# Two transposes of an adaLN, attention and gated-FFN kernel, moved from matrix products to DMA transposes

## The chip, the cores and the metric

The kernel runs on one core of one Trainium2 chip. The metric is device microseconds (us) of one execution; three runs of the kernel before are shown. One more execution was taken by the hardware profiler, and every row below is from it.

## The reference

One transformer block over 2048 rows of 512 numbers: attention of 32 heads that share one key and one value head of 16 numbers, then a bilinear gated unit of width 1792, each behind a layer norm whose scale and shift come from a conditioning vector `c`.

```python
mod = (_silu(c) @ w_mod).reshape(c.shape[0], 6, 1, -1)
sa, ca, ga, sb, cb, gb = (mod[:, 0], mod[:, 1], mod[:, 2], mod[:, 3], mod[:, 4], mod[:, 5])
h = _layernorm(x, axis=-1) * (1 + ca) + sa
x = x + ga * _A_ref(h, A_wq, A_wk, A_wv, A_wo)
h = _layernorm(x, axis=-1) * (1 + cb) + sb
x = x + gb * _B_ref(h, B_w_gate, B_w_up, B_w_down)
...
scores = jnp.einsum("bhqd,bkd->bhqk", q, k) * (Dh ** -0.5)
p = _softmax(scores, axis=-1)
...
g = jnp.einsum("bsd,df->bsf", x, w_gate)
u = jnp.einsum("bsd,df->bsf", x, w_up)
h = g * u
return jnp.einsum("bsf,fd->bsd", h, w_down)
```

## The kernel before

Attention is cut into 32 units: 8 blocks of 256 rows (called sb) by 4 groups of 8 heads. A unit has 16 turns, one for each 128 keys. In a turn TensorE makes four score products (`sc`, lines 657 and 659), ScalarE takes four exponentials of 128x512 (line 661), and TensorE then multiplies them with the values in eight products (`pv`, line 670; these eight open a row of the timeline, so the distance between two such rows is the length of a turn). Every product that keeps numbers exact enough is split into fp16 halves, high and low.

A softmax needs each row's maximum before its exponentials. So the scores are made twice: first as `mx` products (line 601), four in a turn, each reduced by VectorE to a maximum (line 605, `mpart`). These run ahead: 30 steps of maxima are taken before the first exponential (`LEAD`), two more steps go with every turn, and unit u needs its first 24 + 32u. So the last maximum of a unit is taken six steps, three turns, ahead of that unit's first score. In between lies a chain, here called the chain of the maxima: `max_fin` reduces to `mm` (128x16, line 622); `max_rows` turns `mm` by a product with the identity (line 629), splits it in fp16 halves on ScalarE and VectorE (lines 634, 635) and sends it by two small DMAs into rows 48 and 49 of each half of the unit's stationary tile `sst` (line 639).

The linear layers are worked off beside attention, as side groups (line 511): q projections, then for each block of rows the output projection `wo_work`, the gate and up products of `ffn_work` (14 groups with one output tile each) and the down products. A turn takes 4 or 8 half-height side products (the orders `FEW` and `MANY`) or none (`NO_SIDE`, where no group may start). What is not done when attention ends is done behind it, at full height.

`wo_work` ends each 128-row tile by adding x, and by the second norm: statistics on VectorE, the inverse deviation on GpSimd, and `nrm`, which writes the normalised rows `n2` (by GpSimd for blocks 2 to 5, line 769; by ScalarE else, line 771). `ln2_work` then turns `n2` by eight 128x128 products with the identity, four to a turn (line 805), lets ScalarE apply scale and shift, which now are per partition (`hf`, line 813), and lets GpSimd split in halves into `h2T` (lines 818, 819; VectorE for the last block). Only then is block sb put into `h2done`, and only then may its ffn groups start.

Order: each engine runs its instructions in program order, and the program is written in ticks, two to a turn; `after(n, f)` writes f's instructions n ticks later. SyncE (SP) issues all DMAs in one such order; an issue that waits for its data holds up those behind it.

Of the kernel before, what the change touches and what calls it, by code (L numbers as in the profile page):

```python
# [16 lines left out]
OP = mybir.AluOpType  # L17
# [14 lines left out]
SQ_GAP = 2.6  # L32
LAG = 2
ROW_LAG = 4
SLOTS = (0, 1, 2, 3, 6, 7)
SUM_GAP = 4.0
SUM_LAG = 3
SPLIT_GAP = 2.5
# [3 lines left out]
NBANK = 8  # L42
QPRE = 24
Q_LAG = 8
TR_WAIT = 11
NHF = 12
M_STEP = 23
PAIRED = 14
# [15 lines left out]
def adaln_mqa_glu_kernel(ctx: ExitStack, tc: tile.TileContext, x_in, wq_in, wk_in, wv_in, wo_in,  # L64
# [159 lines left out]
    kwb = big.tile([128, 2 * FT * D], F16, name="kwb", tag="wd")  # L224
    hfs = kwb[:, 0:2 * NHF * BT].bitcast(F32).rearrange("p (n t) -> p n t", n=NHF)
    ssqs = [kwb[:, 2 * n * BT:2 * n * BT + 2 * F].bitcast(F32) for n in (KC, 2 * KC)]
    kng = kwb[:, 2 * NHF * BT:2 * NHF * BT + BT]

    def hf(b, k):
# [390 lines left out]
    def max_fin(u):  # L620
        mms[u] = work.tile([128, 2, 8], F32, name="mm")
        nc.vector.tensor_reduce(mms[u], mparts[u], axis=AX.X, op=OP.max)

    def max_rows(u):
        def f():
            mms[u, "b"] = ps_hold("mxt")
            p = mms[u, "b"][0:16, 0:128]
            mms[u, "p"] = p
            nc.tensor.transpose(p, mms[u].rearrange("p a c -> p (a c)"), ident)  # L629

        def g():
            p = mms[u, "p"]
            mt = [work.tile([16, 128], F16, name=f"mt{hl}") for hl in range(2)]
            nc.scalar.activation(mt[0], p, AF.Copy, scale=1.0 / 32.0)
            nc.vector.scalar_tensor_tensor(mt[1], p, 1.0 / 32.0, mt[0], op0=OP.mult, op1=OP.subtract)
            ps_give(mms[u, "b"])
# [85 lines left out]
            timers.setdefault(tick[0] + delay, []).append(f)  # L722

    x1s = {}
    n2s = {}
    n2f = {}

    def load_x(t):
# [6 lines left out]
    def wo_work(sb):  # L735
        on_pool = 2 <= sb < NS - 2

        def op(t):
            def f(i):
                ch, term = divmod(i, 3)  # L740
                ol, wl = TERMS[term]
                return [(och[sb, ch][:, ol, t * 128:(t + 1) * 128], wo[:, wl, ch, :])]
            return f

        def fin(t):
            row = 2 * sb + t

            def f(p):
                x1 = x1s[row]
                nc.vector.scalar_tensor_tensor(x1, p, sca[:, 7:8], x1, op0=OP.mult, op1=OP.add)  # L750
                s2 = work.tile([128, 1, 2], F32, name="st2", bufs=5)
                bs = work.tile([128, 6], F32, name="bs", bufs=4)
                nb = work.tile([128, 2], F32, name="nb", bufs=4)
                yt = {}

                def spread():
                    nc.vector.bn_stats(bs, x1)

                def aggr():
                    nc.vector.bn_aggr(s2[:, 0, :], bs)  # L760
                    yt["y"] = rstd_of(s2, 1)
                    if not on_pool:
                        nc.gpsimd.tensor_tensor(nb[:, 0:1], s2[:, 0, 0:1], yt["y"], op=OP.mult)
                        nc.gpsimd.tensor_scalar(nb[:, 1:2], nb[:, 0:1], -1.0, 0.0, op0=OP.mult, op1=OP.add)

                def nrm():
                    n2 = work.tile([128, D], F32, name="n2", tag="n2", bufs=2)
                    if on_pool:
                        nc.gpsimd.tensor_scalar(n2, x1, s2[:, 0, 0:1], yt["y"], op0=OP.subtract, op1=OP.mult)
                    else:  # L770
                        nc.scalar.activation(n2, x1, AF.Identity, bias=nb[:, 1:2], scale=yt["y"])
                    n2s[row] = n2

                after(3, spread)
                after(4, aggr)
                n2f[row] = nrm
                if t == 1:
                    late = 3 if sb < 2 else 0
                    for j in range(2):
                        after((4, 9)[j] + late, n2f[2 * sb + j])  # L780
                    if sb < NS - 1:
                        after(TR_WAIT + late, lambda: turns.extend(ln2_work(sb)))
# [6 lines left out]
    turns = deque()  # L789
    glus = []  # L790

    def ln2_work(sb):
        st = {}

        def tr(i):
            def f():
                if not h2s:
                    h2T = big.tile([128, 2, 2, KC, ST], F16, name="h2T", tag="wq")
                    glus.append(big.tile([128, 2, 2, FT, ST], F16, name="glu", tag="big"))
                    h2s.update({s: h2T[:, s % 2] for s in range(NS)})  # L800
                st["p"] = ps_hold("mx")
                for k in range(2):
                    for t in range(2):
                        c = k * ST + t * 128
                        nc.tensor.transpose(st["p"][:, c:c + 128],  # L805
                                            n2s[2 * sb + t][:, (2 * i + k) * 128:(2 * i + k + 1) * 128], ident)
            return f

        def ev(i):
            def f():  # L810
                hf = work.tile([128, 2, ST], F32, name="hf", tag="g", bufs=2)
                for k in range(2):
                    nc.scalar.activation(hf[:, k, :], st["p"][:, k * ST:(k + 1) * ST], AF.Identity,  # L813
                                         bias=hsc[:, 2 * i + k, 0:1], scale=hsc[:, 2 * i + k, 1:2])
                ps_give(st["p"])
                eng = nc.vector if sb == NS - 1 else nc.gpsimd
                h = h2s[sb][:, :, 2 * i:2 * i + 2, :]
                eng.tensor_scalar(h[:, 0], hf, 1.0, 0.0, op0=OP.mult, op1=OP.add)
                eng.tensor_tensor(h[:, 1], hf, h[:, 0], op=OP.subtract)
                if i == 1:  # L820
                    (after if sb == 0 else lambda d, f: f())(3, lambda: h2done.add(sb))
            return f

        return [(900, tr(i), ev(i)) for i in range(2)]

    W = {}
    hsc = consts.tile([128, KC, 2], F32, name="hsc")
# [65 lines left out]
    def late_weights():  # L893
# [16 lines left out]
        def m2():  # L910
            st["p"] = ps_mx()
            mod_cols(st["row"][0:64, :], modT[1], st["p"])
            md = dram.tile([2, D], F32, name="md")
            nc.sync.dma_start(md, st["row"][64:128:32, :])
            st["md"] = md

        gab = work.tile([128, D], F32, name="gab", tag="x1", bufs=6)
        gbb = consts.tile([128, D], F32, name="gbb")

        def m3():  # L920
            nc.sync.dma_start(gab, st["md"][0:1, :].to_broadcast([128, D]))
            nc.sync.dma_start(gbb, st["md"][1:2, :].to_broadcast([128, D]))

        items = []
        sl = list(wslices())
# [5 lines left out]
        def stage(n):  # L931
            if "d" in W:
                t = work.tile([128, D], F32, name="wsl", tag="xl", bufs=3)
            else:
                t = hfs[:, SLOTS[taken[0] % len(SLOTS)], :]
                taken[0] += 1
            nc.sync.dma_start(t[:, :sl[n][3]], sl[n][2])
            st[n] = t
# [94 lines left out]

        def inverse():
            nc.vector.reciprocal(sca[:, 0:5], st["t"][:, 0:5])
            nc.vector.tensor_scalar(hsc, modT[1][:, :, 0:64:32], sca[:, 4:5], None, op0=OP.mult)
            nc.gpsimd.tensor_scalar(gab, gab, sca[:, 3:4], 0.0, op0=OP.mult, op1=OP.add)

        def last_column():
# [73 lines left out]

    wlist, dlist, mod_rows = late_weights()
    NSTEP = 32
    later = {}
    mstep = [0, 0]

    def drain_posts():
# [8 lines left out]
    def max_half(a):  # L1128
# [14 lines left out]
            max_parts(u + 1)  # L1143
        if last:
            max_fin(u)
            (_, f, g), = max_rows(u)
            later[min(mstep) + 1] = (f, g)

    def late_max():
        for at in [m for m in later if m <= min(mstep)]:  # L1150
            f, g = later.pop(at)
            f()
            posts.append(g)
            return True
        return False

# [27 lines left out]
    qs = deque(q_proj(b, ch) for b in range(NB) for ch in ((2, 3, 0, 1) if b == 0 else range(KC)))  # L1184
    for n in range(LEAD):
        drain_posts()
        late_max()
# [30 lines left out]
    def attend(u, kt):  # L1218
# [10 lines left out]
        def end_turn(kt):  # L1229
# [7 lines left out]
            if v >= 0:  # L1237
                pv(*divmod(v, KT))
                if v % KT == KT - 1:
                    ends.append(lambda: pv_out(u - 1))  # L1240
            if not late_max() and turns and all(q.ended() for q in qs):
                _, f, post = turns.popleft()
                f()
                posts.append(post)
            hooks(u, 2 * kt + 1)

        for turn in range(2):
# [4 lines left out]
            for j, (what, a) in enumerate(order):  # L1252
                if j == len(order) // 2:
                    drain_posts()
                    if style is not NO_SIDE:
                        late_max()
# [103 lines left out]


# [15 lines left out]
```

## Time and profile before

| what | value |
|---|---|
| median of 3 runs | 1665.59 us (1664.72 to 1666.26) |
| span of the profiled execution | 1663.8 us |
| what lies around the span, against the median | 1.8 us |
| TensorE matmul busy | 1643.3 us, 99% |
| VectorE busy | 1402.3 us, 84% |
| ScalarE busy | 1234.8 us, 74% |
| GpSimd busy | 523.5 us, 31% |
| share of the chain that ended last | PE 93%, ACT 2%, DVE 2%, DMA 1% |

The page gives the span of the profiled execution, from its first to its last instruction; its time as the runs are timed is not shown, and is put here at the span and the 1.8 us. Engines: PE is TensorE, DVE VectorE, ACT ScalarE, POOL GpSimd, SPq the DMA issues of SyncE. Busy time of PE counts overlapping products once.

### The profile page before, as it was taken

How to read it: one execution, taken by the hardware profiler on the slowest of the kernel's cores; microseconds unless marked ns; L12 is line 12 of the kernel's file. 1: busy time of each engine (PE TensorE's matmuls, PEld its weight loads, DVE VectorE, ACT ScalarE, POOL GpSimd, SP SyncE). 2: the span in 40 equal slices, each digit the busy share in tenths (PEclk: the TensorE clock that was granted, in tenths of full speed). 3: DMA queues.
4: the chain of work that ended last, by engine and by line, in shares of the span. 5: the costliest groups of instructions: out<-in, count | busy, mean ns of one | idle time of the engine just before them, and what ended most of it. 6: DMA issues, size and time to landing. Idle time of an engine off the chain costs nothing.

```text
span 1663.8 us, 39821 instructions
## 1 busy us (share of the span) xinstructions
PE 1643.3 (99%) x15677; PEld 747.1 (45%) x15677; DVE 1402.3 (84%) x2434; ACT 1234.8 (74%) x2389; POOL 523.5 (31%) x833
## 2 busy tenths in 40 slices
PE   8899999999999999999999999999999999999999
PEld 4333333355533554335543355434545345454776
DVE  7999999998998999899998999999998999980211
ACT  5688888888777877777877787777878777877300
POOL 4857537864841111301112011300113001210322
PEclk9999999999999999999999999999999999999999
DMA  6313313342210001000000000000000000000100
GB/s 237 108 59 100 95 43 120 96 129 80 77 51 24 18 12 32 19 32 20 20 26 23 25 13 24 26 25 26 20 29 15 26 22 20 26 14 21 33 13 14
DMA packets 66024, 75.39 MB, mean 45 GB/s; under 512 B 17702, under 2 KB 46634, under 8 KB 65836
## 3 DMA queue, kind: packets, MB, share of 16 engines
q1 hardware_dynamic: 63724, 72.26, 13.7%
q8 instruction: 123, 2.02, 0.5%
q10 hardware_dynamic: 2112, 0.59, 0.1%
q14 instruction: 65, 0.53, 0.1%
HBM read 55.51 MB, written 17.04 MB: 44 GB/s over the span
## 4 chain that ended last, share of the span: by engine, by line
PE 93%; ACT 2%; DVE 2%; DMA 1%; issue 1%; POOL 0%; SPq 0%; ACTq 0%; DVEq 0%
PE side L511 41%; PE pv L670 30%; PE mx L601 8%; PE sc L659 8%; PE sc L657 3%; ACT P L661 2%; DVE mpart L605 1%; DMA xbig<-in_A_x_dram 1%; PE mx L805 1%; PE mxt L629 0%; ACT hf L813 0%; PE sc L601 0%; DVE bs L248 0%; DMA kwb<-in_B_w_down_dram 0%; DMA wkv<-in_A_wv_dram 0%
## 5 line engine op out<-in xcount | busy, mean ns | idle before, releaser
L605 DVE TENSOR_REDUCE mpart<-mx 128x1 f32<-128x512 f32 x2016 | 1274.1, 684 | 104.0 <-PE mx L601 95.7
L661 ACT ACTIVATE P<-sc 128x512 f32<-128x512 f32 x2048 | 1094.8, 598 | 274.2 <-PE sc L659 226.9
L601 PE MATMUL mx<-kst,sst 48*128 48x512 f16 x2032 | 631.5, 377 | 3.8 <-ACT P L661 1.7
L659 PE MATMUL sc<-sst,kst 50*128 50x512 f16 x1792 | 597.5, 379 | 0.6 <-ACT P L661 0.3
L670 PE MATMUL pv<-P,vst 128*32 128x512 f32 x4096 | 545.3, 605 | 0.7
L511 PE MATMUL side<-h2T,wg 64*128 64x256 f16 (+1 forms) x2396 | 540.8, 271 | 0.1
L511 PE MATMUL side<-h2T,wu 64*128 64x256 f16 (+1 forms) x2396 | 538.7, 270 | 0.0
L511 PEld LDWEIGHTS <-wg 64*128 64x128 f16 (+1 forms) x2396 | 226.0, 94 | 230.5 <-ACT P L661 194.0
L511 PE MATMUL side<-wd,glu 64*128 64x512 f16 (+1 forms) x1172 | 272.8, 378 | 0.2 <-ACT P L661 0.2
L850 POOL TENSOR_SCALAR glu<-gf 128x256 f16<-128x256 f32 x112 | 45.8, 409 | 671.3 <-DVE gf L849 583.9
L511 PEld LDWEIGHTS <-wu 64*128 64x128 f16 (+1 forms) x2396 | 226.4, 94 | 43.0 <-issue 7.8
L601 PEld LDWEIGHTS <-sst 48*128 48x128 f16 x2064 | 189.9, 94 | 34.2 <-issue 17.4
L659 PEld LDWEIGHTS <-kst 50*128 50x128 f16 x1792 | 162.9, 94 | 63.0 <-issue 50.3
L511 PEld LDWEIGHTS <-glu 64*128 64x128 f16 (+1 forms) x1172 | 98.5, 94 | 192.4 <-ACT P L661 85.9
L670 PEld LDWEIGHTS pv<-P,vst 128*32 128x32 f32 x4096 | 80.7, 108 | 160.9 <-issue 150.1
L849 DVE TENSOR_TENSOR gf<-side,g 128x256 f32<-128x256 f32 x112 | 46.7, 418 | 79.8 <-ACT g L847 77.7
L657 PE MATMUL sc<-sst,kst 50*128 50x256 f16 x512 | 96.9, 268 | 0.1
L511 PE MATMUL side<-h,wq 64*128 64x512 f16 (+1 forms) x372 | 95.0, 376 | 0.4 <-ACT P L661 0.4
L847 ACT ACTIVATE g<-side 128x256 f32<-128x256 f32 x112 | 42.3, 379 | 65.6 <-PE side L511 65.3
L511 PE MATMUL side<-wo,och 64*128 64x512 f16 (+1 forms) x360 | 86.3, 377 | 0.0
L851 POOL TENSOR_TENSOR glu<-gf,glu 128x256 f16<-128x256 f32 x112 | 75.3, 673 | 9.3
L706 POOL TENSOR_TENSOR oc<-oc,rr 128x256 f32<-128x256 f32 x31 | 22.7, 731 | 146.6 <-DMA rr<-ri 100.4
(233 smaller groups left out, 865.4 us busy)
## 6 DMA issues: line engine op xcount, KB each, us to landing
pd<-ev SPq DMA_DIRECT2D x32, 256.0 KB
kwb<-in_B_w_gate_dram SPq DMA_DIRECT2D x32, 224.0 KB
kwb<-in_B_w_up_dram SPq DMA_DIRECT2D x32, 224.0 KB
sst<-qd SPq DMA_DIRECT2D x180, 32.0 KB
qd<-q SPq DMA_DIRECT2D x16, 256.0 KB
oc<-pd SPq DMA_DIRECT2D x64, 64.0 KB
rr<-ri SPq DMA_DIRECT2D x64, 64.0 KB
x<-in_A_x_dram SPq DMA_DIRECT2D x14, 256.0 KB
```

The costliest lines, as they stand in the source:

```text
L511: return nc.tensor.matmul(self.p[:, c * w:(c + 1) * w], left[rows], right[rows], start=start and c == 0, stop=stop and c == len(terms) - 1)
L601: nc.tensor.matmul(m, s[64 * a:64 * a + 48, t // 2, p, t % 2 * 128:(t % 2 + 1) * 128], w[64 * a:64 * a + 48, :], start=(i == 0), stop=(i = ...
L605: nc.vector.tensor_reduce(part, m, axis=AX.X, op=OP.max)
L657: nc.tensor.matmul(t[:, c * ST:(c + 1) * ST], keys, s[64 * a:64 * a + 50, c, p, :], start=True, stop=True)
L659: nc.tensor.matmul(t.rearrange("k (c n) -> k c n", c=2), keys, s[64 * a:64 * a + 50, :, p, :], start=True, stop=True)
L661: ex = nc.scalar.activation(ptl[u, kt, p, a], t, AF.Exp)
L670: nc.tensor.matmul(pvb[u][32 * j:32 * j + 32, :], vst[:, kt, :], ptl[u, kt, p, a], start=(kt == 0), stop=(kt == KT - 1))
L706: eng.tensor_tensor(o, o, st["r"], op=OP.mult)
L847: nc.scalar.activation(g, p[:, 0:ST], AF.Copy, scale=2.0 ** -45)
L849: nc.vector.tensor_tensor(gf, p[:, ST:2 * ST], g, op=OP.mult)
L850: nc.gpsimd.tensor_scalar(glu()[:, 0, f, :], gf, 1.0, 0.0, op0=OP.mult, op1=OP.add)
L851: nc.gpsimd.tensor_tensor(glu()[:, 1, f, :], gf, glu()[:, 0, f, :], op=OP.subtract)
```

## The change

The rows of the second norm are scaled and shifted as they lie, with the scale and shift spread over all partitions (`cbb`, `sbb`, two more broadcast loads), and split in halves, by GpSimd (VectorE for the last block); the halves of 128 rows (128x1024, fp16) are then turned by one DMA transpose straight into `h2T`. `mm` is split in halves by VectorE and turned by one DMA transpose of 128x128 (32 columns used), from where the two small DMAs go on. No product, no ScalarE instruction and no PSUM bank is left in either. Two of six staging slots for weights move, and the scratch for software DMAs shrinks.

```diff
-SLOTS = (0, 1, 2, 3, 6, 7)
+ROWS_LAG = 2
+SLOTS = (0, 1, 2, 3, 12, 13)
...
-TR_WAIT = 11
+TR_LAG = 4
+H2_LAG = 3
...
     def max_rows(u):
-        def f():
-            mms[u, "b"] = ps_hold("mxt")
-            p = mms[u, "b"][0:16, 0:128]
-            mms[u, "p"] = p
-            nc.tensor.transpose(p, mms[u].rearrange("p a c -> p (a c)"), ident)
-
-        def g():
-            p = mms[u, "p"]
-            mt = [work.tile([16, 128], F16, name=f"mt{hl}") for hl in range(2)]
-            nc.scalar.activation(mt[0], p, AF.Copy, scale=1.0 / 32.0)
-            nc.vector.scalar_tensor_tensor(mt[1], p, 1.0 / 32.0, mt[0], op0=OP.mult, op1=OP.subtract)
-            ps_give(mms[u, "b"])
+        m, c = mms[u].rearrange("p a c -> p (a c)"), mtc[:, u % 2, :]
+        nc.vector.tensor_scalar(c[:, 0:16], m, 1.0 / 32.0, None, op0=OP.mult)
+        nc.vector.scalar_tensor_tensor(c[:, 16:32], m, 1.0 / 32.0, c[:, 0:16], op0=OP.mult, op1=OP.subtract)
+        t = mtT[:, u % 2, :]
+
+        def rows():
             s = sst[u % 3]
             for hl in range(2):
-                nc.sync.dma_start(s[48 + hl:113 + hl:64].rearrange("p c q n -> p (c q n)"), mt[hl])
-        return [(100, f, g)]
+                nc.sync.dma_start(s[48 + hl:113 + hl:64].rearrange("p c q n -> p (c q n)"), t[16 * hl:16 * hl + 16, :])
+
+        after(1, lambda: nc.sync.dma_start(t, c, transpose=True))
+        after(1 + ROWS_LAG, rows)
...
+                    eng = nc.vector if sb == NS - 1 else nc.gpsimd
                     if on_pool:
-                        nc.gpsimd.tensor_scalar(n2, x1, s2[:, 0, 0:1], yt["y"], op0=OP.subtract, op1=OP.mult)
+                        eng.tensor_scalar(n2, x1, s2[:, 0, 0:1], yt["y"], op0=OP.subtract, op1=OP.mult)
                     else:
                         nc.scalar.activation(n2, x1, AF.Identity, bias=nb[:, 1:2], scale=yt["y"])
-                    n2s[row] = n2
+                    eng.tensor_tensor(n2, n2, cbb, op=OP.mult)
+                    eng.tensor_tensor(n2, n2, sbb, op=OP.add)
+                    n16 = work.tile([128, 2, D], F16, name="n16", tag="gf", bufs=4)
+                    eng.tensor_scalar(n16[:, 0, :], n2, 1.0, 0.0, op0=OP.mult, op1=OP.add)
+                    eng.tensor_tensor(n16[:, 1, :], n2, n16[:, 0, :], op=OP.subtract)
+                    after(TR_LAG + (3 if sb < 2 else 0), lambda: ln2_turn(sb, t, n16))
...
-    def ln2_work(sb):
...
+    def ln2_turn(sb, t, n16):
...
+        to = h2s[sb].rearrange("p l k n -> p (l k) n")[:, :, t * 128:(t + 1) * 128]
+        nc.sync.dma_start(to, n16.rearrange("p l d -> p (l d)"), transpose=True)
+        if t == 1:
+            after(H2_LAG + (3 if sb < 2 else 0), lambda: h2done.add(sb))
...
-            if not late_max() and turns and all(q.ended() for q in qs):
-                _, f, post = turns.popleft()
-                f()
-                posts.append(post)
...
     run(wo_work(NS - 1))
-    cover(6000)
-    run_items(ln2_work(NS - 1))
     cover(1e9)
```

ScalarE's order in unit 17 (the turn of block 3 falls into it), before: the exponentials `P` of line 661 with what stands between them, up to the unit's evacuation `ev`.

```order
L661 ACTIVATE P<-sc 128x512 x28
L847 ACTIVATE g<-side 128x256
L661 ACTIVATE P<-sc 128x512 x12
L813 ACTIVATE hf<-mx,hsc 128x256 x2
L661 ACTIVATE P<-sc 128x512 x4
L813 ACTIVATE hf<-mx,hsc 128x256 x2
L661 ACTIVATE P<-sc 128x512 x4
L634 ACTIVATE mt_15014<-mxt 16x128
L661 ACTIVATE P<-sc 128x512 x16
L676 ACTIVATE ev<-pv,evs 128x512
```

The same unit of the change, whose line 664 is the exponentials and line 829 `g`:

```order
L664 ACTIVATE P<-sc 128x512 x24
L829 ACTIVATE g<-side 128x256
L664 ACTIVATE P<-sc 128x512 x12
L829 ACTIVATE g<-side 128x256
L664 ACTIVATE P<-sc 128x512 x12
L829 ACTIVATE g<-side 128x256
L664 ACTIVATE P<-sc 128x512 x16
L679 ACTIVATE ev<-pv,evs 128x512
```

The five instructions between exponentials that served the two transposes are gone; the `g` of the side groups have moved by a few turns.

SP's order of DMA issues at the same place, before: the loads of the quotients (`oc`, `ri`, `rr`), of the q rows for a later unit (`sst<-qd`) and of the maxima of unit 18 (`sst<-mt`).

```order
L690 DMA oc<-pd_14409 64x1x256 x2
L695 DMA ri_14634<-rc 128x16
L700 DMA rr<-ri_14634 64x1x256 x2
L566 DMA sst_129<-qd_3_3796 16x4x256 x6
L639 DMA sst_128<-mt_15014 2x8x128
L639 DMA sst_128<-mt_15015 2x8x128
L679 DMA pd_15178<-ev 128x512
```

And of the change:

```order
L693 DMA oc<-pd_14237 64x1x256 x2
L698 DMA ri_14482<-rc 128x16
L703 DMA rr<-ri_14482 64x1x256 x2
L803 DMA_TRANSPOSE h2T<-n_14478 128x8x128
L569 DMA sst_129<-qd_3_3787 16x4x256 x6
L803 DMA_TRANSPOSE h2T<-n_14623 128x8x128
L642 DMA_TRANSPOSE mtT<-mtc 128x128
L640 DMA sst_128<-mtT 2x8x128 x2
L682 DMA pd_15056<-ev 128x512
```

Two transposes of `h2T`, which wait for GpSimd, now stand ahead of the q rows and of the maxima, and the maxima's two DMAs stand behind a transpose of their own.

Where block 0's ffn groups may start (`h2done`), the change writes it five ticks later: eight turns of order `NO_SIDE` instead of four stand there, and with four fewer `MANY` turns 32 half-height side products go behind attention.

## Rows read from the trace of the kernel before

**Rows 1.** The page, part 1: busy us, share of span, instructions.

```profile
PE 1643.3 (99%) x15677; PEld 747.1 (45%) x15677; DVE 1402.3 (84%) x2434; ACT 1234.8 (74%) x2389; POOL 523.5 (31%) x833
```

**Rows 2.** Window, one block: length, PE, PEld, DVE, ACT, POOL busy, PEclk, DMA share, GB/s.

```profile
617.86:805.03 187.17, 187.01 (x1868) 82.85 (x1865) 171.37 (x288) 146.35 (x280) 30.80 (x54) 1.00 0.08 23
```

**Rows 3.** Timeline of PE around block 2's turn: start us, duration us, engine, line.

```profile
685.97 1.07 PE L670 MATMUL pv<-P,vst 128*32 128x512 f32 x8
688.81 1.06 PE L670 MATMUL pv<-P,vst 128*32 128x512 f32 x8
689.80 0.65 PE L805 MATMUL mx<-ident,n 128*128 128x128 f32 x4
692.58 1.06 PE L670 MATMUL pv<-P,vst 128*32 128x512 f32 x8
```

**Rows 4.** Groups by line: busy us, mean ns of one | idle before, releaser.

```profile
L813 ACT ACTIVATE hf<-mx,hsc 128x256 f32<-128x256 f32 x32 | 16.2, 561 | 9.9 <-PE mx L805 9.7
L635 DVE SCALAR_TENSOR_TENSOR mt<-mxt,mt 16x128 f16<-16x128 f32 x32 | 8.8, 276 | 2.8 <-ACT mt L634 2.6
```

**Rows 5.** Timeline of PE in the last turns before unit 29.

```profile
1403.76 1.07 PE L670 MATMUL pv<-P,vst 128*32 128x512 f32 x8
1404.76 0.28 PE L629 MATMUL mxt<-ident,mm 128*16 128x128 f32 x1
1406.81 1.06 PE L670 MATMUL pv<-P,vst 128*32 128x512 f32 x8
1409.72 1.07 PE L670 MATMUL pv<-P,vst 128*32 128x512 f32 x8
```

**Rows 6.** Timeline of PE in the last turns before unit 3, beside q projections.

```profile
194.43 1.06 PE L670 MATMUL pv<-P,vst 128*32 128x512 f32 x8
197.27 1.07 PE L670 MATMUL pv<-P,vst 128*32 128x512 f32 x8
199.77 1.06 PE L670 MATMUL pv<-P,vst 128*32 128x512 f32 x8
```

**Rows 7.** Timeline of PE in the four turns without side work.

```profile
310.02 1.06 PE L670 MATMUL pv<-P,vst 128*32 128x512 f32 x8
312.49 1.06 PE L670 MATMUL pv<-P,vst 128*32 128x512 f32 x8
...
321.47 1.07 PE L670 MATMUL pv<-P,vst 128*32 128x512 f32 x8
```

**Rows 8.** Timeline of PE behind attention.

```profile
1578.44 1.04 PE L805 MATMUL mx<-ident,n 128*128 128x128 f32 x8
...
1579.31 0.27 PE L511 MATMUL side<-h2T,wg 128*128 128x256 f16 x1
...
1579.42 0.27 PE L511 MATMUL side<-h2T,wu 128*128 128x256 f16 x1
```

**Rows 9.** Timelines of DVE and SP: the chain of the maxima of unit 29.

```profile
1403.93 0.22 DVE L622 TENSOR_REDUCE mm<-mpart 128x16 f32<-128x64 f32 x1
...
1405.36 1.19 SPq L639 DMA_DIRECT2D sst<-mt  x2
```

**Rows 10.** Timeline of SP: a store of 256 KB and the load that waits for it.

```profile
1137.41 0.34 SPq L679 DMA_DIRECT2D pd<-ev  x1
1139.42 0.57 SPq L686 DMA_DIRECT2D rc<-pd  x1
```

**Rows 11.** The chain that ended last: its longest DMA inside attention (start, length).

```profile
393.53 4.23 DMA kwb<-in_B_w_down_dram
```

**Rows 12.** Groups by line, GpSimd.

```profile
L769 POOL TENSOR_SCALAR n<-x,st,ry 128x512 f32<-128x512 f32 x8 | 16.7, 2084 | 0.0
L819 POOL TENSOR_TENSOR h2T<-hf,h2T 128x512 f16<-128x512 f32 x14 | 16.3, 1163 | 1.2
```

**Rows 13.** Timelines of POOL and DVE in block 3: norm, and unit 18's `mm`.

```profile
874.85 2.09 POOL L769 TENSOR_SCALAR n<-x,st,ry 128x512 f32<-128x512 f32 x1
...
891.92 0.22 DVE L622 TENSOR_REDUCE mm<-mpart 128x16 f32<-128x64 f32 x1
```

More of the change, by code (lines that the diff above doesn't have):

```diff
@@ L226, in adaln_mqa_glu_kernel @@
     ssqs = [kwb[:, 2 * n * BT:2 * n * BT + 2 * F].bitcast(F32) for n in (KC, 2 * KC)]
+    stg = kwb.bitcast(F32).rearrange("p (n t) -> p n t", t=BT)
     kng = kwb[:, 2 * NHF * BT:2 * NHF * BT + BT]
@@ L780, in f @@
                         after((4, 9)[j] + late, n2f[2 * sb + j])
-                    if sb < NS - 1:
-                        after(TR_WAIT + late, lambda: turns.extend(ln2_work(sb)))
             return f
@@ L788, in adaln_mqa_glu_kernel @@
     h2done = set()
-    turns = deque()
     glus = []
-    def ln2_work(sb):
[L793 to L824, printed above, removed]
+    def ln2_turn(sb, t, n16):
+        if not h2s:
+            h2T = big.tile([128, 2, 2, KC, ST], F16, name="h2T", tag="wq")
+            glus.append(big.tile([128, 2, 2, FT, ST], F16, name="glu", tag="big"))
+            h2s.update({s: h2T[:, s % 2] for s in range(NS)})
+        to = h2s[sb].rearrange("p l k n -> p (l k) n")[:, :, t * 128:(t + 1) * 128]
+        nc.sync.dma_start(to, n16.rearrange("p l d -> p (l d)"), transpose=True)
+        if t == 1:
+            after(H2_LAG + (3 if sb < 2 else 0), lambda: h2done.add(sb))
     W = {}
-    hsc = consts.tile([128, KC, 2], F32, name="hsc")
+    cbb = consts.tile([128, D], F32, name="cbb")
+    sbb = consts.tile([128, D], F32, name="sbb")
     cmx = consts.tile([128, 6], F32, name="cmx")
@@ L912, in m2 @@
             mod_cols(st["row"][0:64, :], modT[1], st["p"])
-            md = dram.tile([2, D], F32, name="md")
-            nc.sync.dma_start(md, st["row"][64:128:32, :])
+            md = dram.tile([4, D], F32, name="md")
+            nc.sync.dma_start(md, st["row"][0:128:32, :])
             st["md"] = md
@@ L920, in m3 @@
         def m3():
-            nc.sync.dma_start(gab, st["md"][0:1, :].to_broadcast([128, D]))
-            nc.sync.dma_start(gbb, st["md"][1:2, :].to_broadcast([128, D]))
+            for j, t in enumerate((sbb, cbb, gab, gbb)):
+                nc.sync.dma_start(t, st["md"][j:j + 1, :].to_broadcast([128, D]))
         items = []
@@ L934, in stage @@
             else:
-                t = hfs[:, SLOTS[taken[0] % len(SLOTS)], :]
+                t = stg[:, SLOTS[taken[0] % len(SLOTS)], :]
                 taken[0] += 1
@@ L1035, in inverse @@
             nc.vector.reciprocal(sca[:, 0:5], st["t"][:, 0:5])
-            nc.vector.tensor_scalar(hsc, modT[1][:, :, 0:64:32], sca[:, 4:5], None, op0=OP.mult)
+            nc.gpsimd.tensor_scalar(cbb, cbb, sca[:, 4:5], sca[:, 4:5], op0=OP.mult, op1=OP.add)
+            nc.gpsimd.tensor_scalar(sbb, sbb, sca[:, 4:5], 0.0, op0=OP.mult, op1=OP.add)
             nc.gpsimd.tensor_scalar(gab, gab, sca[:, 3:4], 0.0, op0=OP.mult, op1=OP.add)
@@ L1115, in adaln_mqa_glu_kernel @@
     NSTEP = 32
-    later = {}
     mstep = [0, 0]
@@ L1145, in max_half @@
             max_fin(u)
[L1146 to L1151, printed above, removed]
-            f()
-            posts.append(g)
-            return True
-        return False
+            max_rows(u)
     fill = deque()
@@ L1254, in attend @@
                     drain_posts()
-                    if style is not NO_SIDE:
-                        late_max()
                     hooks(u, 2 * (kt + turn))
```

8 lines of the change are left out of this document (4 added, 4 removed).

## The prediction

> **What bounds the kernel now.** The page first: TensorE is busy 1643 us of 1664 [rows 1], so whatever leaves its path without putting a wait there comes off the time. Busy time of pipelined products is no proof, so I cut the span into blocks. Over one block of four units TensorE is busy 187.0 of 187.2 us and VectorE 171.4 [rows 2]: VectorE has 8% of room, ScalarE 22%, GpSimd 84%. The timeline then shows the unit of account, the turn: from one `pv` row to the next 2.84 us [rows 3]. A turn that holds four products of the second norm's turn is 3.77 us long (688.81 to 692.58), and one with the maxima's product is 3.05 us (1403.76 to 1406.81) [rows 3, 5]. Where few or no side products stand, a turn is 2.47 to 2.50 us [rows 6, 7]. The sum below is of such differences.
>
> The profiled span is 1663.8 us; the median of the runs is 1665.6. I make the sum against the span and add the 1.8 us that lie between.
>
> **The second norm's turn.** Blocks 1 to 6 have two such turns each, 12 in all. Four products alone are not 0.93 us: they begin at 689.80 and are modelled for 0.65 us [rows 3]. The rest is ScalarE: two `hf` evacuations of 561 ns [rows 4] stand in its order between the exponentials, so the next values products wait for their exponentials. Both leave with the change, and the turn should fall to 2.84: 12 x 0.93 = 11.2 us. Nothing comes back on TensorE or ScalarE.
>
> Behind attention the last block's eight products open a gap of 0.87 us between side products (1578.44 to 1579.31) [rows 8]. Side products of block 6 stand behind it in plenty: eight gate and up groups of 24 products and two down groups, and the former alone, at 0.11 us a product [rows 8], are 21 us of cover for VectorE's eight instructions (each 1.2 us at most by GpSimd's row, under 10 us [rows 12]) and a transpose. So 0.9 us, with nothing given back.
>
> Block 0 differs. Its two turns fall among four turns without side work, which take 11.45 us together (310.02 to 321.47); one without products takes 2.47 [rows 7]. The change writes eight such turns, and four full ones (2.91 us at most as read in [rows 5], 1406.81 to 1409.72) fewer. Before: 11.45 + 4 x 2.91 = 23.1 us. After: 8 x 2.47 = 19.8 us, and 32 half-height side products later on, which behind attention are 16 full-height pairs, 16 x 0.22 = 3.5 us: 23.3 us. A loss of 0.2 us.
>
> **The maxima's turn.** Of 32 units, 27 have it in a turn of full length: 3.05 - 2.84 = 0.21 us each, 5.7 us. Four early ones, beside q projections, cost 0.34 us (2.84 against 2.50) [rows 6]. There VectorE sets the turn, and the change leaves it two small instructions where it had one (276 ns [rows 4]); the gain there is between nothing and 1.4 us, I take 0.7. Unit 0's lies ahead of attention, and I give it nothing.
>
> **What is added.** VectorE: per unit one more instruction of 16 columns, 0.28 us by the row of its like [rows 4], 9 us over the kernel, in turns where it waits for TensorE anyhow; less 171.4 + 1.1 of 184.5 us a block. GpSimd: per 128 rows three more 512-column instructions, less its share of the old split. By [rows 12] a tile takes 2.08 us and four times 1.16 us, 6.7 us, two tiles 13.4 us in a block of 187 us; nothing waits for it early, since from block 1 on the order has the former block's groups between: 43 ticks or more, some 60 us at half a turn each, from the last tile of `wo_work` to the block's first ffn group. Two more broadcast loads, the two small GpSimd instructions and the moved staging slots lie ahead of attention or in GpSimd's idle time: nothing.
>
> **The one cost that the trace does not show** is the DMA transpose, call it L from issue to landing. It decides through the chain of the maxima. For unit 29: `mm` starts at 1403.93 [rows 9]; with its 0.22 us and two small instructions at 0.28, the halves are ready at 1404.7. Then L, then the two small DMAs, whose issues take 1.19 us together (the second starts 0.6 after the first) [rows 9], and landing, 2.0 us by the row of a store and its dependent load [rows 10]. So the rows stand at 1407.3 + L. The unit's first score comes behind the `pv` of 1409.72, 1.0 us after its start as the product of 1404.76 after its own `pv`: 1410.7, and 0.2 sooner with the shorter turn. No wait as long as L is under 3.2 us. The early units have shorter turns: the same steps from 194.6 end at 198.0 + L against 200.5 [rows 6], so under 2.5 us there.
>
> Lower bound for L: nothing speaks for less than the 2.0 us of a whole 256 KB store up to the issue that depends on it [rows 10], since the transpose moves 32 KB but in short pieces. Upper bound: the longest DMA in the chain of waits, 4.2 us [rows 11]. I take 2.0, as the nearer in kind: 32 KB with nothing from HBM, at a time when the DMA queues are almost idle (8% busy) [rows 2]. At 2.0 there is no wait; at 4.2 each of 28 units waits 1.0 us and three wait 1.7, 33 us.
>
> Here a page of the Trainium skill speaks against the change. "VectorE: DVE Perf Modes", section "The three transpose paths", puts a 128x128 transpose at 390 ns on TensorE and 1309 ns by DMA, and its rules say to use TensorE where a PSUM destination will do. Judged by duration that rule would keep the products; here the products stand on the busy path and the DMA does not, and with its 1.3 us for L the chain would have 1.9 us of room: the same sum. No row of this case shows a DMA transpose.
>
> **The sum.** 11.2 + 0.9 - 0.2 + 5.7 + 0.7 = 18.3 us. 1663.8 - 18.3 = 1645.5 us of span, 1647.3 us of time.
>
> **Rivals.**
>
> *The transposed maxima come late* (slower). Place: the first score of every unit, where TensorE has nothing else in its order. Over 3.2 us of L each further us costs 28 to 31 us in all. It cancels the gain where 28 (L - 3.2) + 3 (L - 2.5) = 18.3, at L = 3.7 us. At the upper bound of 4.2: 1647.3 + 33 = 1680 us. For it: nothing in the trace bounds a transpose's landing below 3.7 but likeness. Against it: the two DMAs of which rows show issue and dependent issue stay at 2.0. Chance 0.14; and 0.06 for L between 2.5 and 3.7, 1648 to 1664 us.
>
> *SP's order holds the maxima up.* The second `h2T` transpose waits for GpSimd and stands right ahead of `mtT` in six blocks. In block 3 GpSimd starts the norm at 874.85; with 13.4 us and a `glu` pair of 1.1 it is done at 889.3, and `mm` of the next unit begins at 891.92, 1.9 us sooner with the two shorter turns: halves ready at 890.8 [rows 3, 12, 13]. An issue of 0.6 us [rows 9] is through by then. If 128x1024 is issued as eight blocks of that price, 4.8 us, SP is 3.3 us late, the chain's room of 1.2 us is eaten, and 2 us are lost in six or seven units: 1661 us. On that, "DMA: Bandwidth & Descriptors" of the Trainium skill, in its table on issue times, has the sequencer's time for a transpose within SBUF grow with the number of tiles; no row here shows it. Chance 0.07.
>
> *VectorE is the bound of the maxima's turn.* `mm`, two splits and the four maxima then set it, and the product's 0.21 us were hidden behind them: the 6.4 us for the maxima are not had, 1653.7 us. For it: 92% busy [rows 2]. Against it: the turn with the product is longer by just the product. Chance 0.07.
>
> **How the numbers follow.** My forecast, 1647.3 us, has chance 0.66; its own range is 1642 (ScalarE's and VectorE's small waits for the product go too) to 1652. Faster by over 0.2%, which is about 3.3 us and about what a measurement here can tell from no change: forecast, VectorE and SP cases and most of the small L case, 0.82. Within 0.2%: 0.04. Slower: 0.14. The range runs from 1641 to 1664, which leaves out the late maxima and a little below.
>
> **What would show it.** Right: no turn of 3.77 us, turns of the maxima at 2.84 to 2.9, ScalarE busy 25 us less, `mtT` landing inside 2.5 us, and no wait of TensorE at a unit's first score for a DMA. Wrong: a gap ahead of each unit's first score released by the DMA into `sst` (late maxima); SP rows of line 803 several us long with `mtT` behind them; turns of 3.05 us without a product in them, with VectorE busy throughout.

## The result: slower by 0.45%, and the profile after

The changed kernel takes 1673.19 us (median of 5 runs, 1672.39 to 1673.69), the kernel before in the same series 1666.26 us: a ratio of 1.0045 (95% interval 1.0034 to 1.0055). The forecast was 1647.3 us with a range up to 1664, so the prediction was wrong, in size and in sign. The profiled execution has a span of 1671.9 us against 1663.8.

The page of the changed kernel, busy time by engine (as [rows 1]), and the head of its chain that ended last, as shares of the span:

```profile
PE 1638.7 (98%) x15533; PEld 736.7 (44%) x15533; DVE 1409.5 (84%) x2469; ACT 1215.0 (73%) x2325; POOL 561.3 (34%) x864
...
PE 89%; DVE 5%; ACT 2%; POOL 2%; DMA 1%; issue 1%; SPq 0%; ACTq 0%; DVEq 0%; POOLq 0%
```

TensorE is busy 4.6 us less and ScalarE 20 us less, VectorE 7 us and GpSimd 38 us more, and the span is 8.1 us longer. In the chain TensorE has fallen from 93% to 89%, VectorE has risen from 2% to 5%, and GpSimd is new in it with 2%. So time was not added as work on TensorE but as waits for VectorE and GpSimd, and, as shown below, as turns at a lower clock behind such waits.

Where the 8.1 us lie comes from the timeline. Both kernels have the same 510 turns, so each turn can be set against its counterpart (distance between two `pv` rows, after minus before), and the differences added up by kind:

| part of the span | forecast, us | measured, us |
|---|---|---|
| ahead of the first turn | 0 | +0.6 |
| 12 turns of the norm, blocks 1 to 6 | -11.2 | -10.9 |
| unit 5, turns 6 to 15 (block 0's norm) | -3.3 | +8.2 |
| turns of the maxima, units 0 to 8, and the turn behind it in unit 2 | -1.8 | +7.2 |
| turns of the maxima, later units | -4.6 | +0.8 |
| all other turns | 0 | -2.0 |
| behind attention | +2.6 | +4.2 |
| sum | -18.3 | +8.1 |

The first gain is there in full. This is the timeline of PE in block 2 of the changed kernel, where no turn of 3.77 us is left (the counterpart of [rows 3]):

```profile
701.26 1.06 PE L673 MATMUL pv<-P,vst 128*32 128x512 f32 x8
704.10 1.06 PE L673 MATMUL pv<-P,vst 128*32 128x512 f32 x8
706.93 1.07 PE L673 MATMUL pv<-P,vst 128*32 128x512 f32 x8
```

**First loss: a stop of 10 us.** The timeline of PE in unit 5, where [rows 7] shows the four turns without side work (`mx` is a product of the maxima; in brackets the idle time before it and its releaser):

```profile
325.08 1.06 PE L673 MATMUL pv<-P,vst 128*32 128x512 f32 x8
...
336.90 0.58 PE L604 MATMUL mx<-kst,sst 48*128 48x512 f16 x1 [10.02 <-DMA sst<-qd]
...
338.27 1.94 PE L673 MATMUL pv<-P,vst 128*32 128x512 f32 x8
341.95 1.75 PE L673 MATMUL pv<-P,vst 128*32 128x512 f32 x8
```

TensorE waits for the q rows of the next unit (`sst<-qd`). The eight values products behind the stop take 1.94 us instead of 1.06. The windows say why (length, busy us of PE, PEld, DVE, ACT and POOL, then the granted clock PEclk, DMA share, GB/s):

```profile
195.00:200.00 5.00, 3.49 (x26) 0.86 (x22) 4.90 (x9) 3.27 (x8) 4.07 (x5) 1.00 0.03 7
200.00:203.00 3.00, 3.00 (x13) 0.48 (x14) 1.78 (x4) 0.72 (x2) 0.00 (x0) 0.51 0.42 97
...
336.90:343.30 6.40, 6.40 (x28) 1.12 (x28) 3.68 (x8) 3.26 (x6) 5.90 (x9) 0.50 0.69 189
```

Behind the stop the clock is granted at 0.50, its lower level of 1.2 GHz; it fell at 329.7, inside the stop, and rose at 343.4. The first two windows are unit 2, where a stop of 1.5 us is followed by the same fall, from 200.0 to 203.5. What made SP late is seen on SP itself, in its timeline of DMA issues:

```profile
313.03 0.39 SPq L919 DMA_DIRECT2D kwb<-in_B_w_up_dram  x1
328.69 1.08 SPq L703 DMA_DIRECT2D rr<-ri  x2
329.81 0.46 SPq L553 DMA_DIRECT2D qd<-q  x1
330.37 1.40 SPq L803 DMA_TRANSPOSE h2T<-n  x1
331.81 1.14 SPq L919 DMA_DIRECT2D kwb<-in_B_w_up_dram  x1
333.00 2.77 SPq L569 DMA_DIRECT2D sst<-qd  x6
```

From 313.4 to 328.7 SP issues nothing. In the view of waits the load of `rr` waits 10.9 us for GpSimd's `q` (line 550): `rr` reuses a buffer of the q projections, and the store of `q` right behind it needs the same instruction. GpSimd's timeline in that stretch:

```profile
312.97 1.28 POOL L775 TENSOR_TENSOR n<-n,cbb 128x512 f32<-128x512 f32 x1
...
316.39 1.16 POOL L779 TENSOR_TENSOR n<-n,n 128x512 f16<-128x512 f32 x1
317.53 0.64 POOL L1062 TENSOR_SCALAR kwb<-kwb,sca 128x448 f32<-128x448 f32 x1
...
322.27 1.27 POOL L775 TENSOR_TENSOR n<-n,cbb 128x512 f32<-128x512 f32 x1
...
325.68 1.16 POOL L779 TENSOR_TENSOR n<-n,n 128x512 f16<-128x512 f32 x1
326.81 0.62 POOL L549 TENSOR_SCALAR q<-qf 128x512 f16<-128x512 f32 x1
327.51 1.15 POOL L550 TENSOR_TENSOR q<-qf,q 128x512 f16<-128x512 f32 x1
```

GpSimd has hardly a gap here (14.09 us busy of the 15.00 from 310 to 325): it is still scaling and splitting weights (lines 1062 to 1064), and the change has put two norm tiles of 4.3 us each ahead of the split of `q`. The 8.7 us go through `q`, `rr` and the q rows to TensorE.

**Second loss: VectorE's small splits.** The stop of TensorE in unit 2, then VectorE and GpSimd there:

```profile
198.71 0.37 PE L604 MATMUL mx<-kst,sst 48*128 48x512 f16 x1 [1.51 <-DVE mpart L608]
```

```profile
195.87 0.22 DVE L625 TENSOR_REDUCE mm<-mpart 128x16 f32<-128x64 f32 x1
196.13 1.04 DVE L633 TENSOR_SCALAR mtc<-mm 128x16 f16<-128x16 f32 x1
197.20 0.85 DVE L634 SCALAR_TENSOR_TENSOR mtc<-mm,mtc 128x16 f16<-128x16 f32 x1
```

```profile
195.99 1.14 POOL L928 TENSOR_TENSOR kwb<-kwb 128x448 f32<-128x448 f32 x1
197.09 0.94 POOL L926 TENSOR_TENSOR kwb<-kwb 128x448 f32<-128x448 f32 x1
```

From unit 9 on each split takes 0.17 us. Here each ends just after a GpSimd instruction that began before it (197.17 against 197.13, 198.05 against 198.03). In units 2, 4, 7 and 8, while GpSimd works on weights, six of the eight take 0.58 to 1.17 us. The reduction ahead of them always takes 0.22 us. The Trainium skill, page "SBUF — State Buffer", section "Who interferes with whom", has VectorE and GpSimd share one pair of SBUF ports: an instruction of VectorE with two SBUF inputs, or in a mode that uses both ports, waits for the GpSimd instruction that holds it, and one with at most one SBUF input outside these modes does not. The trace fits that rule, and the run mm_psum below tests it. Not all of unit 2's 3.3 us is the wait itself: in q_early, one of the runs below, the same stop of 1.50 us stands there, the clock stays at 1.00 behind it, and the unit loses 1.8 us.

**Third: no gain in the later turns of the maxima.** The turn ahead of unit 29, 3.05 us with the product in it [rows 5], is now 3.18 us without one:

```profile
1409.32 1.06 PE L673 MATMUL pv<-P,vst 128*32 128x512 f32 x8
1412.50 1.06 PE L673 MATMUL pv<-P,vst 128*32 128x512 f32 x8
```

VectorE there, and the windows of this turn before and after (VectorE's busy time is the third after the length):

```profile
1409.49 0.22 DVE L625 TENSOR_REDUCE mm<-mpart 128x16 f32<-128x64 f32 x1
1409.75 0.17 DVE L633 TENSOR_SCALAR mtc<-mm 128x16 f16<-128x16 f32 x1
1409.96 0.17 DVE L634 SCALAR_TENSOR_TENSOR mtc<-mm,mtc 128x16 f16<-128x16 f32 x1
1410.05 1.28 DVE L608 TENSOR_REDUCE mpart<-mx 128x1 f32<-128x512 f32 x2
```

```profile
1403.76:1406.81 3.05, 3.05 (x36) 1.69 (x34) 3.00 (x7) 2.38 (x6) 0.00 (x0) 1.00 0.01 1
1409.32:1412.50 3.18, 3.15 (x30) 1.25 (x28) 3.08 (x9) 2.33 (x5) 0.00 (x0) 1.00 0.07 15
```

The three small instructions keep VectorE from its maxima for 0.6 us. VectorE is busy 3.08 of the 3.18 us.

**What held.** The transpose itself was fast enough. SP's timeline in unit 17:

```profile
901.68 1.12 SPq L642 DMA_TRANSPOSE mtT<-mtc  x1
903.97 1.18 SPq L640 DMA_DIRECT2D sst<-mtT  x2
```

From issue to the issue that depends on it are 2.29 us; between 2.2 and 2.4 us in 27 of 32 units. TensorE waits for the rows of the maxima 0.8 us in the whole kernel.

### The profile page after: what moved, and what is told of

Read it like the earlier page. It is cut to its first block, busy times and chain, and to the rows that moved or that the text cites. A ratio compares the mean times of both kernels' runs of the same rounds, so it can differ in the third digit from the quotient of the medians.

```text
span 1671.9 us, 39487 instructions
## 1 busy us (share of the span) xinstructions
PE 1638.7 (98%) x15533; PEld 736.7 (44%) x15533; DVE 1409.5 (84%) x2469; ACT 1215.0 (73%) x2325; POOL 561.3 (34%) x864
## 4 chain that ended last, share of the span: by engine, by line
PE 89%; DVE 5%; ACT 2%; POOL 2%; DMA 1%; issue 1%; SPq 0%; ACTq 0%; DVEq 0%; POOLq 0%
PE side L514 39%; PE pv L673 29%; PE mx L604 8%; PE sc L662 8%; DVE mpart L608 3%; PE sc L660 3%; ACT P L664 1%; DMA xbig<-in_A_x_dram 1%; PE sc L604 0%; DVE mtc L633 0%; PE part L282 0%; DVE bs L251 0%; PE pk L290 0%; DMA wkv<-in_A_wv_dram 0%; PE misc L883 0%
## 5 line engine op out<-in xcount | busy, mean ns | idle before, releaser
L514 PE MATMUL side<-wd,glu 64*128 64x512 f16 (+1 forms) x1169 | 267.9, 378 | 0.4 <-ACT P L664 0.4
```

What stands on the lines that cost most here:

```text
L514: return nc.tensor.matmul(self.p[:, c * w:(c + 1) * w], left[rows], right[rows], start=start and c == 0, stop=stop and c == len(terms) - 1)
```

## The experiments

### The halves of the change apart: norm_only and max_only

norm_only is the changed kernel with the maxima of before; max_only is the reverse, the kernel before with `max_rows` of the change:

```diff
-            max_rows(u)
+            (_, f, g), = max_rows(u)
+            later[min(mstep) + 1] = (f, g)
```

```diff
-            (_, f, g), = max_rows(u)
-            later[min(mstep) + 1] = (f, g)
+            max_rows(u)
```

> The second norm's half of the change alone: the maxima are turned by a product with the identity as in the kernel before. My theory: the change lost its gain in two places, VectorE's splits of the maxima that wait for GpSimd (units 2, 4, 7, 8) and a stall of 10 us in unit 5 that the second norm's GpSimd work puts on SP. So this kernel keeps the 12 shorter turns (-10.9 us) and the stall with the slower clock behind it (11.7 us), has more left behind attention (+4.2 us, less 3.3 us of turns without side work), and none of the early losses of the maxima: 1664 to 1666 us, no better than the kernel before. Rival (the stall comes from the maxima's transpose on SP, not from the norm): no stall in unit 5, about 1654 us.

> The maxima's half of the change alone: the second norm is turned by products as in the kernel before. My theory: units 2, 4, 7 and 8 lose 1.1 to 3.3 us each to VectorE's splits that wait for GpSimd, 6.6 us together, the later units gain nothing (+0.8 us), since VectorE's instructions and not TensorE's product set their turn: 1673 to 1675 us. No stall of 10 us in unit 5. Rival (the splits cost time only because the norm's GpSimd work is there too): 1662 to 1667 us, by the 4 to 5 us that the product's absence should give.

norm_only: 1664.47 us, ratio 0.9988 (0.9979 to 0.9997). max_only: 1674.80 us, 1.0053 (1.0038 to 1.0068). Both times lie in the expected ranges. Turn by turn norm_only keeps the gain of blocks 1 to 6 and the stop in unit 5 (9.85 us, units 5 to 7 together 5.4 us longer than before). max_only has no stop there, loses 3.1 us in unit 2 and 1.3 in unit 4. That its total fits is in part luck: units 2, 4, 7 and 8 together lose 4.3 us and not 6.6, and the 22 turns of the maxima in units 9 to 30 lose 2.3 us and not 0.8. In units 17, 21, 25 and 29 the first split takes 0.65 to 0.83 us there, beside GpSimd's splits of the second norm into `h2T`, so weights are not the only work of GpSimd that it waits for. The two differences to before, -1.5 and +8.8 us, add up to 7.3 us; the whole change costs 6.9. By this sum the halves hardly touch each other.

### Whose wait is it? mm_psum

```diff
-        mms[u] = work.tile([128, 2, 8], F32, name="mm")
+        mms[u] = ps_mx("mm")[:, 0:16].rearrange("p (a c) -> p a c", a=2)
```

> The changed kernel with the maxima reduced into PSUM instead of SBUF, so that VectorE's two splits each read at most one operand from SBUF; the number of instructions is the same. My theory: the splits of 1.04 and 0.85 us in unit 2, 0.83 and 0.58 in unit 4, 1.17 in units 7 and 8 wait for a GpSimd instruction on its way through the same port; read from PSUM none waits, all take 0.17 to 0.28 us, and units 2, 4, 7, 8 get back 6.6 us: 1666 to 1667.5 us. The stall of unit 5 stays. Rival (they wait for the former transpose of the same buffer, or for the DMA): durations and time as they were, 1672 to 1674 us.

1668.10 us, ratio 1.0012 (1.0003 to 1.0022), 5.1 us below the changed kernel; a little less than expected. The durations decide: the first of the two splits in this run, minimum, median and maximum in ns:

```profile
L633 DVE TENSOR_SCALAR mtc<-mm x32: 173/174/176, 67.9 to 1496.8; 128x16 f16<-128x16 f32 x32
```

In the changed kernel it had 174, 175 and 1172. The second split, which still reads one operand from SBUF, is at 173 to 175. Units 2, 4, 7 and 8 are shorter by 6.1 us together, and the clock stays at 1.00 in unit 2. GpSimd's work, the buffers of the transpose and the DMAs are unchanged, so the rival falls.

### What holds the q rows: q_early, turns_late, norm_late

The three edits of the changed kernel, in this order:

```diff
-QPRE = 24
+QPRE = 16
...
-                    after(TR_LAG + (3 if sb < 2 else 0), lambda: ln2_turn(sb, t, n16))
+                    after(TR_LAG + (12 if sb == 0 else 3 if sb < 2 else 0), lambda: ln2_turn(sb, t, n16))
...
-                    late = 3 if sb < 2 else 0
+                    late = 11 if sb == 0 else 3 if sb < 2 else 0
```

> The changed kernel with the loads of the q rows written four turns sooner (QPRE 16 for 24), so that SP comes to them ahead of what waits for GpSimd. My theory: the wait of 10.0 us of TensorE for these rows in unit 5 is gone, and with it the turns at the lower clock behind it: 11.7 us less, 1661.5 us (1660 to 1663). Rival (the rows wait for something else, such as the transfers of the weights that are under way at that time): the wait stays, 1672 to 1674 us.

1670.54 us, ratio 1.0029 (1.0020 to 1.0039): my number was missed by 9 us. The wait for the q rows is gone. The waits of PE between 300 and 352 us show what came in its place:

```profile
PE sc L662 <- DMA sst<-mtT: 3.7, 1, 3.7
PE side L514 <- POOL wu L1063: 1.0, 1, 1.0
```

SP's issues in this run (lines between them left out):

```profile
327.41 1.08 SPq L703 DMA_DIRECT2D rr<-ri  x2
...
329.10 1.41 SPq L803 DMA_TRANSPOSE h2T<-n  x1
...
332.76 1.52 SPq L803 DMA_TRANSPOSE h2T<-n  x1
...
335.50 1.18 SPq L642 DMA_TRANSPOSE mtT<-mtc  x1
```

SP is still held until 327.4. With the q rows out of the way, the next thing in its queue, the transpose of the maxima, is the late one: VectorE's halves are ready at 330.01, their issue starts at 335.50. Ahead of that wait TensorE waits for weights that GpSimd has not finished. Moving the victim did not take away the cause.

> The changed kernel with block 0's two transposes into h2T written nine ticks later, so that on SP the q rows of the next unit stand ahead of both; GpSimd's order is as it was. My theory: SP was held by GpSimd's split of a q projection, which stands behind the norm's 8.7 us on GpSimd (SP's load of rr waited 10.9 us for it); the transposes cost only their 1.4 us of issue and the weight load next to them. The wait for the q rows shrinks from 10.0 us to 7.4 to 8.6 and stays; some four more turns without side work cost 2 us: 1672 to 1675 us. Rival (the transposes on SP hold the q rows up): the wait goes, 1661 to 1664 us.

> The changed kernel with block 0's norm itself written eight ticks later: SP's order is that of the kernel with late transposes, but on GpSimd the split of the q projection now stands ahead of the norm's two tiles of 4.33 us. My theory: SP's load of rr is let go 8.7 us sooner, TensorE's wait for the q rows shrinks from 10.0 us to 1.5 or less, and with the turns at the lower clock this gives 10 us, less 2 us for four more turns without side work: 1664 to 1667 us. Rival (GpSimd's order does not matter, SP's does): the time of the kernel with late transposes.

turns_late: 1670.23 us, ratio 1.0029 (1.0018 to 1.0039). norm_late: 1663.21 us, 0.9988 (0.9979 to 0.9997). In both SP issues in one and the same order, with the q rows ahead of both transposes. What differs is GpSimd's order, and ScalarE's by block 0's two norm instructions, which move with GpSimd's. The wait in turns_late:

```profile
PE mx L604 <- DMA sst<-qd: 7.6, 1, 7.6
```

In norm_late there is no wait for the q rows at all, and SP gets to `rr` at 319.33 instead of 327.10, since GpSimd starts the split of `q` at 317.44:

```profile
317.44 0.62 POOL L549 TENSOR_SCALAR q<-qf 128x512 f16<-128x512 f32 x1
```

```profile
319.33 1.08 SPq L703 DMA_DIRECT2D rr<-ri  x2
```

So GpSimd's queue is the cause, and the transpose on SP accounts for 2.4 of the 10 us. The total of turns_late is 2 us under the expected range and that of norm_late 0.8 us. One reason is that the four more turns without side work cost less than the 2 us put in for them: in turns_late they are 2.0 us shorter than the same turns of the changed kernel, and the part behind attention is 2.6 us longer.

### The norm where GpSimd has room: block0_products

```diff
+                    if sb == 0:
+                        n2s[row] = n2
+                        return
...
+                    if sb == 0:
+                        after(TR_WAIT + late, lambda: turns.extend(ln2_work(sb)))
```

(The maxima as in norm_only; `ln2_work` of the kernel before, for block 0 alone.)

> The norm's half of the change for blocks 1 to 7 alone: block 0's norm is turned by products as in the kernel before, and so are the maxima. My theory: the loss of block 0 lies in GpSimd, which is full of weights there; the twelve shorter turns of blocks 1 to 6 (-10.9 us) and the gap behind attention (-0.9 us) are then had without it: 1654 to 1656 us. Rival (GpSimd's work in block 1, or the transposes' traffic, costs as much as block 0 did): 1659 to 1664 us.

1656.41 us, ratio 0.9945 (0.9930 to 0.9960), 0.4 us above the expected range and far from the rival's. Units 0 to 8 differ from those of before by 0.3 us in sum, and the gain of the twelve turns is kept. The stop was a matter of block 0, when GpSimd is full of weights.

### The turn of the maxima without VectorE's splits: maxima_gpsimd, both_mended, from_unit_11, late_units_only

```diff
+        if u < GP_FROM:
             nc.vector.tensor_scalar(c[:, 0:16], m, 1.0 / 32.0, None, op0=OP.mult)
             nc.vector.scalar_tensor_tensor(c[:, 16:32], m, 1.0 / 32.0, c[:, 0:16], op0=OP.mult, op1=OP.subtract)
+        else:
+            nc.gpsimd.tensor_scalar(m, m, 1.0 / 32.0, 0.0, op0=OP.mult, op1=OP.add)
+            nc.gpsimd.tensor_scalar(c[:, 0:16], m, 1.0, 0.0, op0=OP.mult, op1=OP.add)
+            nc.gpsimd.tensor_tensor(c[:, 16:32], m, c[:, 0:16], op=OP.subtract)
```

(`GP_FROM` is 9, 10, 11 and 11. In the first three the units below it reduce their maxima into PSUM as in mm_psum. both_mended and from_unit_11 also turn block 0's norm by products; late_units_only does that too, turns the maxima of units 0 to 10 by products, and has one buffer for the columns of the maxima instead of two.)

> The changed kernel with the maxima in PSUM for units 0 to 8 (as in the run of that name) and, from unit 9 on, where GpSimd has no more weights, with the two splits done by GpSimd (three small instructions) instead of VectorE. My theory: from unit 9 on the turn of the maxima is set by VectorE, which has one reduction and two splits of 0.2 us each beside its four maxima; with the splits gone the turn falls from 3.02 to 3.27 us to 2.85 to 2.95, 0.15 to 0.3 us in 22 units: 3.3 to 6 us below the kernel with the maxima in PSUM throughout (1668.1), 1662 to 1665 us. Rival (something else sets these turns, or the later splits make the first scores wait): 1667 us or more.

1669.35 us, ratio 1.0028 (1.0018 to 1.0038): half right. The turn ahead of unit 29 in this run:

```profile
1404.71 1.07 PE L682 MATMUL pv<-P,vst 128*32 128x512 f32 x8
1407.63 1.07 PE L682 MATMUL pv<-P,vst 128*32 128x512 f32 x8
```

It takes 2.92 us. Over the 22 turns of the maxima in units 9 to 30 the mean is 2.89 us, against 3.15 in the changed kernel, 3.02 in mm_psum and 3.11 before. So VectorE did set this turn, and its splits ate what the product gave back. The total is missed by one wait: in unit 8 TensorE waits 5.2 us for the rows of unit 9's maxima, because VectorE's reduction is done at 476.4 and GpSimd, still with weights, starts the splits at 482.86.

> The parts that gained, together: block 0's norm turned by products as in the kernel before, blocks 1 to 7 by DMA transposes; the maxima turned by DMA transposes, reduced into PSUM and split by VectorE in units 0 to 9, and split by GpSimd from unit 10 on (with unit 9 left to VectorE, since there the splits stood 5 us behind GpSimd's weights in the run before). My theory: 1656.4 us of the kernel with block 0's products, less 0.22 us in each of 21 turns of the maxima (3.11 against 2.89 us): 4.6 us, nothing lost in the early units: 1651 to 1653 us. Rival (gains in the maxima's turn are eaten by waits at the first scores, or by GpSimd's norm): 1655 us or more.

1663.41 us, ratio 0.9985 (0.9976 to 0.9994): missed by some 11 us, and the rival named the place. With block 0's norm turned by products, block 1's second norm tile on GpSimd stands in turn 12 of unit 9 and no longer in turn 6, and there it meets unit 10's maxima. GpSimd, then PE:

```profile
524.69 1.16 POOL L793 TENSOR_TENSOR n<-n,n 128x512 f16<-128x512 f32 x1
525.93 0.20 POOL L642 TENSOR_SCALAR mm<-mm 128x16 f32<-128x16 f32 x1
```

```profile
531.70 0.58 PE L672 MATMUL sc<-sst,kst 50*128 50x512 f16 x1 [3.88 <-DMA sst<-mtT]
```

VectorE had finished the reduction at 520.75. This one turn is 5.9 us longer than without the wait. The rest of the 11 us was not traced to a cause, but for some 1.5 us in unit 1 of the profiled execution, at the lower clock (see the last section).

> The kernel of the run before (both mended) with GpSimd's splits from unit 11 on instead of unit 10. My theory of its loss: in unit 9 VectorE had the reduction of unit 10's maxima done at 520.5, but GpSimd was inside block 1's second norm tile until 525.9, so that the rows came behind TensorE's first score, 3.9 us of wait and 2 us of lower clock; nothing else was lost from unit 9 on but three waits of 0.6 us for the maxima's rows. With unit 10 left to VectorE it is 5.9 us less: 1657.5 us (1656 to 1659). Rival (the transposes into h2T hold up the rows on SP or in the DMA queues whoever splits): the wait stays, 1662 to 1664 us.

> Only what gained where it gained: block 0's norm and the maxima of units 0 to 10 are turned by products as in the kernel before; the norm of blocks 1 to 7 and the maxima of units 11 to 31 by DMA transposes, with GpSimd's splits; one buffer for the maxima's columns instead of two. My theory: 1656.4 us of the kernel with block 0's products, less 0.22 us in each of 20 turns of the maxima (4.4 us), plus some three or four first scores that wait 0.6 to 0.9 us for the rows (2.5 us): 1654.5 us (1653 to 1656). Rival (those waits eat all of it): 1656 us or more.

from_unit_11: 1655.41 us, ratio 0.9940 (0.9926 to 0.9954); the long wait is gone, so it was GpSimd's order and not the transposes into `h2T`. It is 0.6 us below the expected range. late_units_only: 1653.19 us (1652.82 to 1653.64), ratio 0.9924 (0.9912 to 0.9937), the fastest of all and as expected, with only one first score that waits (0.6 us). Its page reads:

```profile
PE 1631.0 (99%) x15562; PEld 741.2 (45%) x15562; DVE 1398.4 (85%) x2417; ACT 1216.9 (74%) x2340; POOL 569.2 (34%) x923
...
PE 93%; DVE 3%; ACT 2%; DMA 1%; issue 1%; POOL 0%; SPq 0%; ACTq 0%; DVEq 0%
```

GpSimd does as much as in the changed kernel (569 against 561 us), and is out of the chain.

## Why the prediction was wrong, step by step

- **The second norm's turn, 12 x 0.93 us:** right, 10.9 against 11.2 us, and by the mechanism given.
- **GpSimd's added work, "nothing waits for it early":** this step failed first. The argument was made for blocks 1 and later and holds there; block 0 was left out of it. The added work was weighed against a block in which GpSimd has 84% of room, and not against its load in block 0, where it is busy 14.09 of 15.00 us and a tile adds 4.3 us. The cost was a stop of 10.0 us and the lower clock behind it: unit 5's turns 6 to 15 are 8.2 us longer instead of 3.3 shorter (norm_late, block0_products).
- **VectorE's splits, 0.28 us "by the row of its like":** the second failed step. The row taken had its operand in PSUM; the new instructions read SBUF, and while GpSimd works they wait for it. Over units 0 to 8 the turns of the maxima lose 7.2 us where 1.8 were to be gained; 5 to 6 us of it is that wait, with the lower clock behind it in unit 2 (mm_psum).
- **The maxima's turn, 27 x 0.21 us:** the third. The reading "the turn with the product is longer by just the product" took two things that were both true for one cause. VectorE was busy 3.00 of those 3.05 us too. The rival that VectorE is the bound, given 0.07, is what happened in the later units (maxima_gpsimd), and the sign that the prediction named for it is there: such turns without a product, with VectorE busy.
- **The DMA transpose, L = 2.0 us:** 2.3 measured up to the dependent issue, no wait but 0.8 us, as said. (The Trainium skill's 1309 ns, "VectorE: DVE Perf Modes", section "The three transpose paths", lie below that; the measurement decides.) The rival of late maxima, on which the chance for slower rested, did not come about in the changed kernel. The sign came from elsewhere.
- **SP's order, chance 0.07:** the place was right (transposes that wait for GpSimd ahead of the next unit's rows), but in block 0, for the q rows, and mainly by `rr` and `q`, which stood there before. The issue of eight blocks, put at up to 4.8 us, took 1.24 to 1.30 us in 12 of 16 cases.
- **Behind attention, 3.5 - 0.9 us:** mis-sized. The trace has 43 more full-height side products there, where 32 (16 pairs) were put in, and the part grew by 4.2 us.

Of the 2.0 us that all other turns are shorter, 1.9 lie in two turns of units 6 and 7, which were 3.75 and 4.00 us long. TensorE waited 0.64 and 0.89 us there for exponentials that stood behind ScalarE's work on weights (line 991 of the kernel before), which waited for its DMA; in the changed kernel they are 2.91 and 2.92 us. The forecast had no term for it. What stays open: why that work no longer meets these turns, and the 0.6 us ahead of the first turn, which varies by a us or more from run to run without a change there (78.5 to 80.9 us in these profiles).

## What to carry to other kernels

Before work is moved to an engine that is idle on the mean, look at that engine's timeline at the place where the work lands, and list what stands behind it in its order and in the queues that wait for it; here 8.7 us on an engine that was 31% busy stopped TensorE for 10 us. When a wait is taken from one victim, look for the next in the same queue; only putting the work behind what the queue waits for (norm_late) or taking it away (block0_products) ended it. A product that leaves a turn shortens it only if no other engine is as long: compare the turn with that engine's busy time first.

## What the runs showed of the hardware

- A VectorE instruction on 128x16 in SBUF took up to 1.17 us instead of 0.17 while GpSimd worked; with `mm` in PSUM never more than 0.18 us (mm_psum).
- A DMA transpose within SBUF, which the kernel before does not have: 128x128 takes 1.13 us of issue and 2.3 us up to a dependent issue; 128x1024 takes 1.24 to 1.30 us of issue in 12 of 16 cases, so eight times the data costs 0.1 to 0.2 us more there. Some issues of either took 1.4 to 2.2 us; why was not tried. The Trainium skill, "DMA: Bandwidth & Descriptors", has this time grow with the number of tiles; these rows agree, with 0.1 to 0.2 us for seven more blocks of 128x128.
- A stop of TensorE can cost more than its length: behind the one of 10.0 us the granted clock was 0.50 for 6.5 us, and behind the one of 1.5 us in unit 2 for over 3 us. It does not have to: every profile, that of the kernel before too, has a stop of 1.59 us in unit 1, and in four of the thirteen (norm_only, q_early, both_mended, late_units_only) the clock fell behind it, with 1.5 us more for the unit; in the others it stayed at 1.00. The windows behind this stop in norm_only, and around it in the changed kernel:

```profile
128.95:132.30 3.35, 3.35 (x16) 0.64 (x16) 2.07 (x4) 1.71 (x4) 2.41 (x3) 0.50 0.88 280
126.90:132.40 5.50, 5.16 (x48) 1.75 (x48) 4.61 (x9) 3.94 (x8) 4.71 (x6) 1.00 0.65 193
```

So a difference of 1.5 us between two single profiles can be this alone.
